# A fused attention and Fourier-filter kernel: the order of the prologue's last products, one eviction, the first queries and the first PV batch are rearranged

## The chip, the cores and the metric

The kernel runs on one core of one Trainium2 chip. The metric is the device time of one execution in microseconds. Lower is better. Three runs of the kernel before gave 673.25, 674.58 and 678.07 us, so the median is 674.58 us.

The engines of the core are named as the profile names them: PE is TensorE (matmuls; its weight loads are PEld), ACT is ScalarE, DVE is VectorE, POOL is GpSimd, SP is SyncE, which here issues most DMAs.

## The reference

Two results are computed from two inputs of 2048 rows by 448 columns and concatenated by columns.

```python
# A: attention, 16 query heads of width 28, one shared key and value head
q = (x @ wq).reshape(B, S, 16, 28).transpose(0, 2, 1, 3)
k, v = x @ wk, x @ wv
p = softmax(einsum("bhqd,bkd->bhqk", q, k) * 28 ** -0.5)
a = einsum("bhqk,bkd->bhqd", p, v) ... @ wo
# B: a spectral filter
y = irfft2(rfft2(x) * (w_r + 1j * w_i))
return concatenate([a, y], axis=-1)
```

## The kernel before, in words

The program has a prologue (about the first 71 us of the profiled execution), a branch, and a main loop of 256 steps.

**The prologue.** Queries, keys and values are projected in four column chunks of 512 (`proj`, L298; evicted by ACT into `qraw`, L302). Between the projections stand the first pieces of the Fourier transform: `fft1_fold` on DVE, `fft1_a(q)` (L120: 64 small products into two tiles `pa`, 32 for each `p`, each tile evicted by ACT into `a`, L123), and `fft1_b(q)`, which is `fft1_mm(q)` (L135: 16 products into `pbb` and `po`) followed by `fft1_out(q)` (eviction into `bs`, L143 on ACT or L147 on DVE for q = 7, then a store).

At the prologue's end PE has these left, in this order: `fft1_a(6)`, `fft1_b(5)`, `fft1_a(7)` whole, then small products: `shift(1, NC)` (L239, one product that sums the bounds `prod`), eight transposes of the values (`turn`, L401, into `pv`), four products of one row for the largest bound (L406, `pb3`), eight more transposes, and last `fft1_mm(6)`.

The chain that decides the branch runs over these engines: DVE computes `prod` (L235), PE does `shift`, DVE copies `cvec` (L240) and reduces it to `cmax` (L394), PE does the `pb3` products, DVE reduces them to `bits` (L407). Every engine loads `bits` into a register and branches on it (L412, L413). The branch holds a fallback for bounds over a limit. With this input it is not taken. On the path that is not taken, each of PE, ACT and DVE waits for its own earlier instructions to be done before it goes on.

**The first queries.** `build_q(0, 0, True)` scales the first query tile (`qt`, L185), rounds it (`qh`, L186) and takes the remainder (`ql`, L187), all on DVE. `copy_q` puts `qh` and `ql` into the tile `qa`: four copies of 32 partitions on DVE (L172) and four on ACT (L175). `twice(q, u)` (L165, DVE) then copies 64 partitions of one half u of `qa` to the other 64.

**After the branch.** ACT evicts the values from `pv` to `vs` (L444) and the two tiles of `fft1_mm(6)`. DVE makes the second half of the keys (`keys(1, ...)`, L228 and L229), then parts of the next query tile, and evicts `fft1_mm(7)` (L147).

**The main loop.** Each step makes two score tiles `s` (L694, two products each, three buffers of two PSUM banks), ACT exponentiates each into `p` (L697), and `flush` issues the products of `p` with the values (PV, L676, four for a step). `LAG = 1`: at each odd step `flush(1)` issues all waiting steps but one. So the first PV batch comes at step 3 and holds the steps 0 and 1; every later batch holds two steps as well. Step 0 has `fft1_b(7)` between its scores and those of step 1. `fft1_mm(7)` and the PV tile take the same PSUM buffer (`ps_o`, one buffer).

**What sets the order.** PE's order is the program's order, written by hand (`manual_schedule`). On ACT, DVE, POOL and SP a planner orders the instructions by its own estimate of when each can start; on the chip each engine then runs its list strictly in that order. `behind(a, b)` only fixes that `a` is listed after `b`; it adds no wait. PSUM tiles of the prologue come from a pool of six banks that is closed at the branch, and the score tiles take the same banks.

Of the kernel before, what the change touches and what calls it, by code (L numbers as in the profile page):

```python
# [9 lines left out]
F32 = mybir.dt.float32  # L10
# [3 lines left out]
AF = mybir.ActivationFunctionType  # L14
ALU = mybir.AluOpType
# [8 lines left out]
NC = 4  # L24
# [8 lines left out]
LAG = 1  # L33
# [5 lines left out]
def kernel(ctx: ExitStack, tc: tile.TileContext, t: dict):  # L39
    nc = tc.nc  # L40
# [12 lines left out]
    qraw = cp.tile([128, NG, S], F32, name="qraw")  # L53
    ka = cp.tile([128, S], F32R, name="ka")
    vs = cp.tile([128, 16, 32], F32, name="vs")
    cvec = cp.tile([128, NG, NC], F32, name="cvec")
# [4 lines left out]
    def behind(ins, other):  # L61

        tc.add_manual_dep(ins.ins, other.ins.name,
                          mybir.DependencyInfo(mybir.DependencyClass.NoSync, mybir.DependencyReason.DATA),
                          reason="order of issue")
# [12 lines left out]
    fc, xb, ff = {}, {}, {}  # L78
# [29 lines left out]

    at1, stored = {}, []

    def fft1_a(q):
        f, cs1 = ff.pop(q), fc["cs1"][:113]
        for p in range(2):
            pa = ps1[0].tile([128, 2, DF], F32, name="pa", tag="p")
            for e in range(2):
                for k, (n, o0) in enumerate(((113, 0), (112, 113))):
                    for h in range(2):
                        for r in range(2):
                            r0 = 64 * h + 32 * r
                            mm(pa[r0:r0 + 32, e, o0:o0 + n], f[:, 2 * r + k, 2 * p + e, h], cs1[:, 2 * r + k, :n],  # L120
                               start=True, stop=True)
            a = at1[q, p] = fp.tile([128, 2, DF], F32, name="a", tag=("pwr", "pwi")[p])
            nc.scalar.activation(a, pa, AF.Copy)  # L123
# [37 lines left out]

    qa = {}

    def twice(q, u):
        return nc.vector.tensor_copy(q[64:128, 2 * u:2 * u + 2], q[0:64, 2 * u:2 * u + 2].bitcast(F32))  # L165

    def copy_q(q, qh, ql, after=None, whole=True):

        for u in range(2):
            for i in (2 * u, 2 * u + 1):  # L170
                r = slice(32 * i, 32 * i + 32)
                v = nc.vector.tensor_copy(q[0:32, i], qh[r].bitcast(F32))  # L172
                if after is not None:
                    behind(v, after)
                a = nc.scalar.activation(q[32:64, i], ql[r].bitcast(F32), AF.Copy)  # L175
            if u == 0 or whole:
                v = twice(q, u)
        return a, v

    def build_q(c, g, first=False):  # L180
        cs = slice(c * CW, (c + 1) * CW)
        qt = qp.tile([128, CW], F32, name="qt", bufs=1)
        qh = qp.tile([128, CW], F32R, name="qh", bufs=1)
        ql = qp.tile([128, CW], F32R, name="ql", bufs=1)
        nc.vector.tensor_scalar(qt, qraw[:, g, cs], mask, cvec[:, g, c:c + 1], op0=ALU.mult, op1=ALU.add)  # L185
        nc.vector.tensor_copy(qh, qt)  # L186
        nc.vector.tensor_tensor(ql, qt, qh.bitcast(F32), op=ALU.subtract)  # L187
        if (c, g) not in qa:
            qa[c, g] = qp.tile([128, 4, CW], F32R, name="qa")
        q = qa[c, g]  # L190
        if first:
            return q, qh, ql
        for i in range(4):
            for p, src in enumerate((qh, ql)):
                mv = nc.sync.dma_start(q[32 * p:32 * p + 32, i].bitcast(F32), src[32 * i:32 * i + 32].bitcast(F32))
                behind(mv, stored[-1])
        nc.sync.dma_start(q[64:128].bitcast(F32), q[0:64].bitcast(F32))
# [7 lines left out]
    with tc.tile_pool(name="w1", bufs=1) as w1, tc.tile_pool(name="p1", bufs=6, space=PSUM) as p1:  # L205
# [28 lines left out]
        def terms(c0, c1):  # L234
            return nc.vector.tensor_scalar(prod[:, :, c0:c1], qmx[:, :, c0:c1], kmb, None, op0=ALU.mult)  # L235
# [151 lines left out]
            fetch(range(12, 14), slice(1536, S), nc.gpsimd)  # L387

        fft1_a(6)
        copy_q(*parts, terms(1, NC), False)  # L390
        fft1_b(5)
        fft1_a(7)
        shift(1, NC)
        top = nc.vector.tensor_reduce(cmax, cvec, axis=AX.X, op=ALU.max)  # L394
        behind(twice(parts[0], 1), top)

        pv = p1.tile([128, 16, 32], F32, name="pv", tag="p")

        def turn(bs):
            for b in bs:  # L400
                nc.tensor.transpose(pv[:, b], kf[32:64, b * 128:(b + 1) * 128], ident[32:64, 32:64])  # L401

        turn(range(8))
        pb3 = p1.tile([128, 64], F32, name="pb3", tag="p")
        for g in range(NG):
            mm(pb3[0:1, 4 * g:4 * g + 4], cmax[:, g:g + 1], sel4, start=True, stop=True)  # L406
        nc.vector.tensor_reduce(bits, pb3[0:1, 0:16], axis=AX.X, op=ALU.max)  # L407
        turn(range(8, 16))
        pb6 = fft1_mm(6)


# [1 line left out]
        with tc.If(rv > int(np.float32(BOUND).view(np.int32))), tc.tile_pool(name="g1", bufs=1) as g1:  # L413
            k4 = g1.tile([128, S], F32, name="k4")
            nc.vector.memset(k4, 0.0)
            for i in range(4):
                nc.vector.tensor_copy(k4[32 * i:32 * i + DH], kf[0:DH])
            mz = g1.tile([128, 4, 32], F32, name="mz")
            nc.vector.memset(mz, 0.0)


            qv = qraw.rearrange("p g (b q) -> p (g b) q", q=128)
            banks = [p1.tile([128, 512], F32, name="ps", tag="p") for _ in range(2)]
            with tc.For_i(0, 64, 1) as n:
                qs = g1.tile([128, 128], F32, name="qs")
                nc.vector.tensor_copy(qs, qv[:, bass.ds(n, 1)][:, 0])
                mx = g1.tile([128, 4, 4], F32, name="mx")
                for i in range(4):
                    r = slice(32 * i, 32 * i + 32)
                    for h in range(4):  # L430
                        ps = banks[0]
                        mm(ps, qs[r], k4[r, h * 512:(h + 1) * 512], start=True, stop=True)
                        nc.vector.tensor_reduce(mx[:, i, h:h + 1], ps, axis=AX.X, op=ALU.max)
                nc.vector.tensor_reduce(mz[:, :, DH], mx, axis=AX.X, op=ALU.max)
                pt = banks[1][:, :128]
                mm(pt, mz.rearrange("p i d -> p (i d)"), ident, start=True, stop=True)
                nc.vector.scalar_tensor_tensor(qs, qs, mask, pt, op0=ALU.mult, op1=ALU.add)
                nc.vector.tensor_copy(qv[:, bass.ds(n, 1)][:, 0], qs)
            nc.vector.memset(cvec, 0.0)
            nc.vector.memset(mask, 1.0)  # L440
            on_act, on_dve = copy_q(*build_q(0, 0, True))


        behind(nc.scalar.activation(vs, pv, AF.Copy), on_act)  # L444
        fft1_out(6, pb6, on_act)
        behind(keys(1, nc.vector.tensor_copy), on_dve)

# [220 lines left out]
    step = 0  # L668

    def flush(n, last=False):  # L670
        while len(pend) > n:
            c, g, kc, ps = pend.pop(0)
            if kc == 0:
                po[c, g] = ps_o.tile([128, CW], F32, name="po")
            for i in range(4):
                mm(po[c, g][32 * i:32 * i + 32], vs[:, kc], ps[i // 2][:, i % 2], start=(kc == 0), stop=(kc == 15))  # L676
            if kc == 15:
                o = osb[c, g] = ap.tile([128, CW], F32, name="osb")
                if last:
                    for k in range(4):  # L680
                        s = slice(128 * k, 128 * k + 128)
                        nc.scalar.activation(o[:, s], po[c, g][:, s], AF.Copy)
                else:
                    nc.vector.tensor_copy(o, po[c, g])  # L684
                    for k in range(4):
                        at(max(step + 1, 64 * c + 43) + k, norm, c, g, k)

    for n, (c, g) in enumerate(order):
        for kc in range(16):
            ps = []  # L690
            for u in range(2):
                s = ps_s.tile([128, 2, CW], F32, name="s")
                for j in range(2):
                    last = mm(s[:, j], ka[:, kc * 128:(kc + 1) * 128], qa[c, g][:, 2 * u + j], start=True, stop=True)  # L694
                begun.append(last)
                p = pp.tile([128, 2, CW], F32, name="p")
                nc.scalar.activation(p, s, AF.Exp, scale=SCALE)  # L697
                ps.append(p)
            if kc % 2 == 0:
                for f, a in between.pop(step // 2, []):  # L700
                    f(*a)
            else:
                flush(LAG)
            pend.append((c, g, kc, ps))
            for f, a in later.pop(step, []):
                f(*a)
            if kc == 4 and n + 1 < len(order):
                build_q(*order[n + 1])
            step += 1
# [4 lines left out]
    c = NC - 1  # L714
# [137 lines left out]
```

## Time and profile before

| what | us |
|---|---|
| median of three runs | 674.58 |
| the three runs | 673.25, 674.58, 678.07 |
| the profiled execution, whole | 674.18 |
| its span, first to last instruction | 672.3 |
| from the prologue's last projection to the first score | 64.17 to 71.80 |
| PE busy | 664.3 |
| ACT busy | 529.2 |
| DVE busy | 318.1 |

The profiled execution lies 0.40 us under the median and 1.9 us over its own span. A row of a timeline reads: start in us from the span's start, duration, engine, line, operation, the tile written and the tiles read, how many instructions the row merges, and in brackets how long the engine was idle before it and whom it waited for. A row of a stage table reads: the stretch, its length, and busy time with number of instructions of PE, PEld, DVE, ACT and POOL, then the granted TensorE clock as a share of the full one, the mean busy share of the DMA engines and GB/s.

### The profile page before, as it was taken

Reading aid. Unit: us, or ns where it says so; the run is one execution under the profiler, and the core shown is the slowest. Engines: PE = TensorE matmul, PEld = TensorE weight load, DVE = VectorE, ACT = ScalarE, POOL = GpSimd, SP = SyncE. Lnnn points to the kernel's source line nnn. Section 1 sums busy time; section 2 is a strip of 40 time slices with the busy share of each in tenths; the row PEclk is TensorE's granted clock in tenths of the full one; section 3 lists DMA queues with packets and bytes.
Section 4 is the critical chain, followed back from the end, with each engine's and each line's share of the span. In section 5 each row is a group of like instructions: output and inputs, shape, how many; then the busy total and the mean of one; then the engine's idle time right before and its main releaser. Section 6 shows DMA issues by size and latency. Waiting matters only on the chain.

```text
span 672.3 us, 11826 instructions
## 1 busy us (share of the span) xinstructions
PE 664.3 (99%) x4480; PEld 370.6 (55%) x4480; DVE 318.1 (47%) x769; ACT 529.2 (79%) x607; POOL 62.6 (9%) x113
## 2 busy tenths in 40 slices
PE   9999999999999999999999999999999999999997
PEld 6877544555555555555555555555555555555555
DVE  6999438659895902055332502072614220171513
ACT  4555888888888888888888888888888888888881
POOL 3022261111110000000011100000100100000110
PEclk9999899999999999999999999999999999999999
DMA  8755785555551323030322311020424130120001
GB/s 275 248 169 166 205 208 144 135 142 141 139 145 41 78 82 78 15 77 15 105 72 62 88 49 43 25 65 17 132 58 100 50 76 15 46 59 1 28 29 56
DMA packets 34251, 61.87 MB, mean 92 GB/s; under 512 B 6529, under 2 KB 22802, under 8 KB 33228
## 3 DMA queue, kind: packets, MB, share of 16 engines
q1 hardware_dynamic: 30544, 49.18, 26.4%
q0 software_dynamic: 3072, 11.00, 6.5%
q8 instruction: 36, 0.59, 0.4%
q10 hardware_dynamic: 576, 0.92, 0.4%
q14 instruction: 23, 0.19, 0.1%
HBM read 29.35 MB, written 14.75 MB: 66 GB/s over the span
## 4 chain that ended last, share of the span: by engine, by line
PE 87%; ACT 1%; issue 0%; ACTq 0%
PE s L694 39%; PE po L676 35%; PE pw L596 5%; PE py L558 2%; PE pz L544 2%; ACT p L697 1%; PE s L596 1%; PE pc L463 1%; PE pu L465 0%; PE pc L464 0%; PE pc L465 0%; PE pu L463 0%; PE pu L464 0%; ACT yb L601 0%; PE pbb L135 0%
## 5 line engine op out<-in xcount | busy, mean ns | idle before, releaser
L697 ACT ACTIVATE p<-s 128x1024 f32<-128x1024 f32 x512 | 484.9, 1031 | 96.5 <-PE s L694 96.5
L694 PE MATMUL s<-qa,ka 128*128 128x512 f32 x1024 | 300.4, 415 | 2.1 <-ACT p L697 1.5
L694 PEld LDWEIGHTS s<-qa,ka 128*128 128x128 f32 x1024 | 177.9, 189 | 140.2 <-ACT p L697 114.9
L676 PE MATMUL po<-p,vs 128*32 128x512 f32 x2048 | 246.0, 598 | 0.0
L676 PEld LDWEIGHTS po<-p,vs 128*32 128x32 f32 x2048 | 53.6, 109 | 123.6 <-issue 118.2
L603 DVE COPY ya<-pw 128x448 f32<-128x448 f32 x12 | 7.5, 625 | 145.2 <-PE pw L596 127.7
L584 DVE RECIPROCAL r<-r 128x128 f32<-128x128 f32 x64 | 60.8, 950 | 1.2
L564 DVE TENSOR_TENSOR y<-py,m 128x226 f32<-128x226 f32 x16 | 6.3, 394 | 64.0 <-ACT m L562 64.0
L547 DVE COPY z<-pz 113x512 f32<-113x512 f32 (+1 forms) x16 | 11.1, 692 | 48.6 <-PE pz L544 48.6
L536 POOL DMA_DIRECT2D fi<-fi x8 | 4.4, 551 | 246.2 <-PE pz L544 239.6
L567 POOL TENSOR_TENSOR yo<-y 128x226 f32<-128x226 f32 x16 | 9.3, 583 | 188.4 <-issue 174.6
L298 PE MATMUL pq<-xh,wqh 128*128 128x512 f32 x64 | 26.2, 409 | 0.5 <-ACT wqh L280 0.5
L298 PE MATMUL pq<-xh,wql 128*128 128x512 f32 x64 | 25.3, 396 | 0.1
L491 DVE CAST bh<-b 128x450 fp32r<-128x450 f32 x16 | 6.4, 397 | 38.7 <-PE pu L464 21.1
L302 ACT ACTIVATE qraw<-pq 128x512 f32<-128x512 f32 x16 | 9.2, 600 | 18.0 <-PE pq L298 18.0
L684 DVE COPY osb<-po 128x512 f32<-128x512 f32 x15 | 10.4, 690 | 20.9 <-PE po L676 20.9
L298 PE MATMUL pq<-xl,wqh 128*128 128x512 f32 x48 | 19.1, 397 | 0.0
L583 DVE STREAM_SHUFFLE r<-osb 128x128 f32<-128x128 f32 x64 | 19.0, 297 | 0.1
L585 DVE TENSOR_TENSOR osb<-osb,r 128x128 f32<-128x128 f32 x64 | 18.4, 288 | 1.2
L596 PE MATMUL pw<-woh,ol 128*128 128x448 f32 x51 | 18.8, 368 | 0.0
L596 PE MATMUL pw<-wol,oh 128*128 128x448 f32 x51 | 18.6, 365 | 0.0
L596 PE MATMUL pw<-woh,oh 128*128 128x448 f32 x51 | 18.5, 362 | 0.0
(124 smaller groups left out, 568.3 us busy)
## 6 DMA issues: line engine op xcount, KB each, us to landing
qa<-qa SPq DMA_DIRECT2D x15, 512.0 KB, 4.2
raw<-xa SPq DMA_DIRECT2D x16, 256.0 KB, 5.2
xb<-xb SPq DMA_DIRECT2D x8, 512.0 KB, 3.6
qa<-qh SPq DMA_DIRECT2D x60, 64.0 KB, 2.0
qa<-ql SPq DMA_DIRECT2D x60, 64.0 KB, 2.0
ob<-yo SPq DMA_DIRECT2D x16, 226.0 KB, 2.2
t<-bs SPq DMA_DIRECT2D x16, 225.0 KB, 4.6
wr<-wr POOLq DMA_DIRECT2D x16, 225.0 KB, 4.8
```

Source lines behind the costliest of these rows:

```text
L298: mm(pq, w[:, j, gs], x[:, j], start=(j == 0 and n == 0), stop=(j == 3 and n == 1))
L544: mm(pz[:w, j], c2["c", q][:, j, o0:o0 + w], c2["F", q][:, j], start=True, stop=True)
L547: nc.vector.tensor_copy(z[:w], pz[:w].rearrange("p j (r n) -> p r j n", r=2))
L558: mm(py[:, k], z[:w, r, js], cs3[:w, k], start=True, stop=True)
L583: nc.vector.stream_shuffle(r, o, [DH] * 32)
L584: nc.vector.reciprocal(r, r)
L585: nc.vector.tensor_tensor(o, o, r, op=ALU.mult)
L596: mm(p, x[c][:, g, s], w[:, g], start=(g == 0 and n == 0), stop=(g == NG - 1 and n == 2))
L676: mm(po[c, g][32 * i:32 * i + 32], vs[:, kc], ps[i // 2][:, i % 2], start=(kc == 0), stop=(kc == 15))
L684: nc.vector.tensor_copy(o, po[c, g])
L694: last = mm(s[:, j], ka[:, kc * 128:(kc + 1) * 128], qa[c, g][:, 2 * u + j], start=True, stop=True)
L697: nc.scalar.activation(p, s, AF.Exp, scale=SCALE)
```

## The change

Four edits, in the order of the diff:

- `fft1_a` takes a list of halves, so that the halves p = 0 and p = 1 of `fft1_a(7)` can be issued apart.
- `copy_q` handles one half u at a time; `twice` is called apart from it. `build_q(..., first=True)` makes `qt` and `qh` on ACT; `ql` stays on DVE.
- The prologue's end is reordered. PE's new order: `fft1_b(5)`, `shift(1, NC)`, `fft1_a(7)` half 0, the `pb3` products, all sixteen transposes, `fft1_a(7)` half 1, `fft1_mm(6)`. ACT evicts `vs` before the branch, between the evictions of the two halves of `fft1_a(7)`. `twice(0)` is listed behind `cmax`; `copy_q(1)` and `twice(1)` follow in the program without such a rule.
- `flush(LAG if step > 1 else 0)`: at step 1 the PV products of step 0 are issued. The batch at step 3 then holds step 1 alone. From step 5 on the batches are as before.

```diff
-    def fft1_a(q):
-        f, cs1 = ff.pop(q), fc["cs1"][:113]
-        for p in range(2):
+    def fft1_a(q, ps=range(2)):
+        f, cs1 = ff[q], fc["cs1"][:113]
+        for p in ps:
...
+    def copy_q(u, q, qh, ql):
+        for i in (2 * u, 2 * u + 1):
+            r = slice(32 * i, 32 * i + 32)
+            v = nc.vector.tensor_copy(q[0:32, i], qh[r].bitcast(F32))
+            a = nc.scalar.activation(q[32:64, i], ql[r].bitcast(F32), AF.Copy)
+        return a, v
...
-        nc.vector.tensor_scalar(qt, qraw[:, g, cs], mask, cvec[:, g, c:c + 1], op0=ALU.mult, op1=ALU.add)
-        nc.vector.tensor_copy(qh, qt)
+        if first:
+            nc.scalar.activation(qt, qraw[:, g, cs], AF.Identity, bias=cvec[:, g, c:c + 1], scale=mask)
+            nc.scalar.activation(qh, qt, AF.Copy)
+        else:
+            nc.vector.tensor_scalar(qt, qraw[:, g, cs], mask, cvec[:, g, c:c + 1], op0=ALU.mult, op1=ALU.add)
+            nc.vector.tensor_copy(qh, qt)
...
         fft1_a(6)
-        copy_q(*parts, terms(1, NC), False)
+        ts = terms(1, NC)
+        behind(copy_q(0, *parts)[1], ts)
         fft1_b(5)
-        fft1_a(7)
         shift(1, NC)
         top = nc.vector.tensor_reduce(cmax, cvec, axis=AX.X, op=ALU.max)
-        behind(twice(parts[0], 1), top)
-        pv = p1.tile([128, 16, 32], F32, name="pv", tag="p")
-        def turn(bs):
-            for b in bs:
-                nc.tensor.transpose(pv[:, b], kf[32:64, b * 128:(b + 1) * 128], ident[32:64, 32:64])
-        turn(range(8))
+        behind(twice(0, *parts), top)
+        copy_q(1, *parts)
+        twice(1, *parts)
+        fft1_a(7, (0,))
         pb3 = p1.tile([128, 64], F32, name="pb3", tag="p")
         for g in range(NG):
             mm(pb3[0:1, 4 * g:4 * g + 4], cmax[:, g:g + 1], sel4, start=True, stop=True)
         nc.vector.tensor_reduce(bits, pb3[0:1, 0:16], axis=AX.X, op=ALU.max)
-        turn(range(8, 16))
+        pv = p1.tile([128, 16, 32], F32, name="pv", tag="p")
+        for b in range(16):
+            nc.tensor.transpose(pv[:, b], kf[32:64, b * 128:(b + 1) * 128], ident[32:64, 32:64])
+        nc.scalar.activation(vs, pv, AF.Copy)
+        fft1_a(7, (1,))
         pb6 = fft1_mm(6)
...
-        behind(nc.scalar.activation(vs, pv, AF.Copy), on_act)
...
-                flush(LAG)
+                flush(LAG if step > 1 else 0)
```

In the changed program as it is built, the lists of the engines differ from those before in these places alone. On DVE the part in question reads: `ql`, a copy of `qh`, the reduction of the last `qraw`, a copy of `qh`, `prod`, two copies of `qh`, `twice(1)`, `cvec`, `cmax`, `twice(0)`, `bits`. Its `twice(1)` waits for the last of ACT's four copies of `ql`. On ACT the part reads: the last `qraw`, two copies of `ql`, a tile of `fft1_a(6)`, a copy of `ql`, the other tile of `fft1_a(6)`, a copy of `ql`, two tiles of `fft1_mm(5)`, half 0 of `fft1_a(7)`, `vs`, half 1 of `fft1_a(7)`, the branch. Before, DVE's list read: `prod`, three copies of `qh`, `twice(0)`, a copy of `qh`, `cvec`, `cmax`, `twice(1)`, `bits`.

More of the change, by code (lines that the diff above doesn't have):

```diff
@@ L162, with twice @@
     qa = {}
[L164 to L178, printed above, removed]
+    def copy_q(u, q, qh, ql):
[4 more added lines that the diff above has]
+        return a, v
+    def twice(u, q, *_):
+        return nc.vector.tensor_copy(q[64:128, 2 * u:2 * u + 2], q[0:64, 2 * u:2 * u + 2].bitcast(F32))
     def build_q(c, g, first=False):
@@ L440 @@
             nc.vector.memset(mask, 1.0)
-            on_act, on_dve = copy_q(*build_q(0, 0, True))
-        behind(nc.scalar.activation(vs, pv, AF.Copy), on_act)
+            parts = build_q(0, 0, True)
+            for u in range(2):
+                on_act, _ = copy_q(u, *parts)
+                on_dve = twice(u, *parts)
         fft1_out(6, pb6, on_act)
```

## The prediction

> **What bounds the kernel now.** I read the page first, then the busy time by stage around the branch, then the timelines of PE, ACT and DVE there.
>
> ```profile
> span 672.3 us, 11826 instructions
> ...
> PE 87%; ACT 1%; issue 0%; ACTq 0%
> ```
>
> The chain that ended last is PE's for 87% of the span. The changed lines all run before step 6 of the main loop, that is before about 88 us, and from step 5 on the loop is the same. So the change is worth what it adds or takes on PE's path between the last projection and the first regular PV batch.
>
> ```profile
> 64.78:68.19 3.41, 3.41 (x124) 2.83 (x116) 3.28 (x8) 2.94 (x6) 1.00 (x2) 1.00 0.59 192
> 68.19:71.60 3.41, 3.05 (x54) 2.25 (x45) 1.80 (x6) 3.22 (x8) 0.00 (x0) 1.00 0.13 29
> 71.60:75.02 3.42, 3.22 (x20) 1.95 (x20) 3.15 (x5) 2.66 (x4) 2.74 (x5) 0.50 0.94 222
> 75.02:78.43 3.41, 3.04 (x18) 1.65 (x10) 1.76 (x4) 2.47 (x4) 2.06 (x4) 1.00 1.00 247
> ...
> 75.28:81.47 6.19, 5.64 (x32) 2.36 (x28) 1.54 (x3) 5.42 (x6) 2.06 (x4) 1.00 1.03 293
> ```
>
> The column after the five engines is the granted clock. From 71.60 to 75.02 it is half. The stretch before it, as long, held mostly small products; the one before that held only Fourier products and was followed by the full clock. In the last row PE waits 6.19 - 5.64 = 0.55 us.
>
> ```profile
> 66.70 1.75 PE L120 MATMUL pa<-cs,f 113*32 113x113 f32 x64
> ...
> 68.38 0.39 PE L239 MATMUL pb<-prod,blk 128*128 128x12 f32 x2
> 68.70 0.68 PE L401 MATMUL pv<-ident,kf 32*128 32x32 f32 x8
> 69.33 0.34 PE L406 MATMUL pb<-sel,cmax 128*1 128x4 f32 x8
> 69.61 0.71 PE L401 MATMUL pv<-ident,kf 32*128 32x32 f32 x8
> 70.25 0.41 PE L135 MATMUL pbb<-a,fw 64*64 64x225 f32 x2
> ...
> 70.88 0.36 PE L135 MATMUL po<-a,fw 64*64 64x225 f32 x2
> 71.80 2.04 PE L694 MATMUL s<-qa,ka 128*128 128x512 f32 x4 [0.56 <-ACT vs L444]
> 73.78 0.64 PE L135 MATMUL pbb<-a,fw 64*64 64x225 f32 x2
> ...
> 75.28 1.66 PE L694 MATMUL s<-qa,ka 128*128 128x512 f32 x6
> ...
> 79.62 1.92 PE L676 MATMUL po<-p,vs 128*32 128x512 f32 x16
> ```
>
> From 66.70 to 70.88 + 0.36 = 71.24 PE runs without a gap: 4.54 us. Then 0.56 us pass before the first scores.
>
> **Part by part. First the new wait on PE.** These are ACT's and DVE's rows.
>
> ```profile
> 64.20 0.60 ACT L302 ACTIVATE qraw<-pq 128x512 f32<-128x512 f32 x1 [1.79 <-PE pq L298]
> ...
> 65.77 1.27 ACT L175 ACTIVATE qa<-ql 32x512 fp32r<-32x512 f32 x2
> 67.07 0.55 ACT L123 ACTIVATE a<-pa 128x450 f32<-128x450 f32 x1
> 67.63 1.27 ACT L175 ACTIVATE qa<-ql 32x512 fp32r<-32x512 f32 x2
> ...
> 70.94 0.60 ACT L444 ACTIVATE vs<-pv 128x512 f32<-128x512 f32 x1 [0.16 <-ACTq L413]
> ```
>
> ```profile
> 61.44 0.16 DVE L240 COPY cvec<-pb 128x4 f32<-128x4 f32 x1
> ...
> 62.17 0.69 DVE L103 TENSOR_TENSOR xb<-f 113x512 f32<-113x512 f32 x1
> 62.77 0.54 DVE L185 TENSOR_SCALAR qt<-qraw,mask,cvec 128x512 f32<-128x512 f32 x1
> 63.23 0.42 DVE L104 TENSOR_TENSOR f<-xb 113x256 f32<-113x256 f32 x1
> ...
> 64.57 0.42 DVE L186 CAST qh<-qt 128x512 fp32r<-128x512 f32 x1
> 65.03 0.69 DVE L187 TENSOR_TENSOR ql<-qt,qh 128x512 fp32r<-128x512 f32 x1
> 65.64 0.68 DVE L303 TENSOR_REDUCE qmx<-qraw 128x1 f32<-128x512 f32 x1
> 66.35 0.23 DVE L235 TENSOR_SCALAR prod<-qmx,kmb 128x12 f32<-128x12 f32 x1
> 66.49 1.28 DVE L172 CAST qa<-qh 32x512 fp32r<-32x512 f32 x3
> ...
> 68.83 0.15 DVE L240 COPY cvec<-pb 128x12 f32<-128x12 f32 x1
> 69.02 0.17 DVE L394 TENSOR_REDUCE cmax<-cvec 128x4 f32<-128x16 f32 x1
> 69.22 0.69 DVE L165 CAST qa<-qa 64x1024 fp32r<-64x1024 f32 x1
> 69.94 0.16 DVE L407 TENSOR_REDUCE bits<-pb 1x1 f32<-1x16 f32 x1
> 71.77 0.68 DVE L228 CAST ka<-kf 32x1024 fp32r<-32x1024 f32 x1 [1.67 <-DVEq L413]
> ...
> 76.20 0.62 DVE L147 COPY bs<-po 128x450 f32<-128x450 f32 x1
> ```
>
> The nearest row for `qt` and `qh` on ACT is a copy of the same shape, from the groups by line and form:
>
> ```profile
> L288 ACT ACTIVATE xh<-raw 128x512 fp32r<-128x512 f32 x12 | 7.1, 626 | 0.2
> ```
>
> Without L185 and L186, DVE takes the four folds (64.57 - 63.23 = 1.34 us) right after L103 ends at 62.86, so about 62.92 to 64.26, and `ql` runs 64.26 to 64.95. ACT makes `qt` and `qh` between its evictions before that. `qt` needs the first columns of `cvec`, which are there at 61.60. Two instructions of 0.626 us are 1.25 us, and ACT is idle for 1.79 us ahead of the `qraw` eviction at 64.20. So I take them as hidden, with `qh` done by about 63.7. A scale and a bias read per partition are not in that copy; at 0.9 us each (the two would just fill 1.79) they would still end before `ql` can start. If ACT had not this idle time, their 1.25 us would stand ahead of everything below. DVE then has two copies of `qh` (1.28/3 = 0.43 each) and the reduction (0.68) ahead of `prod`: 64.87 + 0.43 + 0.68 + 0.43 = 66.4, where it is now (66.35). Nothing is gained there.
>
> ACT starts its copies of `ql` at 65.0 and works through four of them and two tiles of `fft1_a(6)`: 4 x 0.635 + 2 x 0.55 = 3.64, so the last ends at about 68.7. DVE's `twice(1)` is listed ahead of `cvec` and waits for that last copy. All of DVE's bound chain is queued behind it. So `twice(1)` runs 68.75 to 69.44, `cvec` starts at 69.4, `cmax` 0.19 later, and it is done at about 69.75, not 69.19. Now `cvec` at 68.83 needs only PE's shift.
>
> PE meanwhile does `shift` when `prod` is done (66.75, 0.32 to the next product by 68.38 and 68.70) and half of `fft1_a(7)` (1.75/2 = 0.88), so it stands at 67.95 before the `pb3` products, which need `cmax`. They start at 69.85: 1.9 us of idle PE that does not exist now. The products left are the same ones as now, so the prologue ends at 71.24 + 1.9 to 1.95, about 73.2, and the first scores come at about 73.75. Bounds: `pb3` follows ACT's last copy by 1.15 us (68.7 to 69.85), and DVE's own copies end at 67.35 (66.49 + 2 x 0.43), so 0.5 us of wait is left even if ACT is no limit; 2.3 if `qt` and `qh` push `ql` by 0.4. I take 1.95, from the rows as they stand.
>
> **`vs` ahead of the branch.** The gap of 0.56 is put down to `vs`, which ends at 70.94 + 0.60 = 71.54; the rest is issue. PE also has its own branch in that gap. In the built program the first scores wait for ACT's path through the branch, which now lies behind the eviction of half 1. ACT passed the branch in 0.16 (its row), DVE in 1.67. I expect at most 0.3 (71.24 to 71.54), at least 0; I take 0, because PE's branch fills it.
>
> **The clock.** Four scores and `fft1_mm(7)` take 75.28 - 71.80 = 3.48 us now. At full clock `fft1_mm` takes 71.24 - 70.25 = 0.99, and four scores about 0.95 (six issue within 1.66, which includes the last one's end). So the half clock costs 3.48 - 1.94 = 1.53. With the change the stretch from 68.19 to 71.60 holds 1.65 us of idle, then `pb3` and sixteen transposes (0.3 + 1.3), and next to nothing dense, less than the stretch that led to half clock now. So I expect half clock from 71.60 again. It then covers half 1 of `fft1_a(7)`, `fft1_mm(6)` (75.28 - 73.78 = 1.50 at half clock against 0.99: 0.5 lost) and the first scores up to 75.02 (0.3 lost): 0.8 plus some for half 1, together 0.95.
> [...]
>
> So step 1's scores start at 75.28 + 1.95 - 1.53 + 0.95 = 76.65, 1.4 later than now.
>
> **The first PV batch.** Four of the eight products of the 1.92 us row move ahead of step 2's scores, while ACT catches up. The 0.55 us of waits can go. Against that, the first PV now comes before DVE has emptied the bank that `fft1_mm(7)` used: 76.82 by the last DVE row, and `bits` is 0.5 later in the change (`twice(0)` 69.75 to 70.44, then `bits`), so about 77.5. Step 1's scores end at 76.65 + 0.95 = 77.6, so this wait is hidden in the forecast; if the clock stays full, the scores end near 76.7 and PE waits 0.8. Bounds -0.55 and +0.3 net; I take -0.5, since the wait is covered.
>
> **Sum.** 1.95 - 1.53 + 0.95 - 0.5 = 0.9 us. On the profiled execution's own 674.18 (672.3 of span and 1.9 around it): **675.1 us**. The median of the runs is 0.40 above that execution, so against 674.58 this is half a microsecond, a change of 0.1%. About 1%, 6.7 us, is what a measurement can tell from no change.
>
> **Rivals.** *ACT's copies are no limit, and the clock stays full* (faster). The wait is 0.5, PE has dense work on both sides of the small products, and 1.53 is gained. `pb3` stands at 68.45, 0.9 before its present 69.33, so `bits` and DVE's work after the branch are 0.9 earlier and L147 ends at 75.9. Step 1's scores start at 75.28 + 0.5 - 1.53 = 74.25 and end at 75.2, so the first PV waits 0.7 for L147 against the 0.55 that goes. Sum: 0.5 - 1.53 + 0.15 = -0.9, 673.3 us; without any wait of PV 672.6. For it: the shorter light part. Against it: 3.64 us of ACT rows. Chance 0.14.
>
> *The wait is there, but no half clock follows.* This rests on the phase of the 3.41 us stretches against the program: if a border falls at 69.7, each side holds about half of the 3.5 us (1.9 + 0.3 + 1.3) light part. Then step 1's scores start at 75.28 + 1.95 - 1.53 = 75.7, the first PV waits 0.8 for DVE against 0.55 of waits that go, and the sum is 0.42 + 0.25 = +0.7: 674.9 us. [...] Chance 0.2.
>
> *A second stretch at half clock* (slower). If the stretch 71.60 to 75.02, with 0.5 us of branch and 64-row products at half speed, also counts as light, half clock lasts to 78.43. It decides where PE's dense share is under what 71.60 to 75.02 has now (3.22 busy). Another 3.41/2 = 1.7 is lost: +2.6, 676.8 us. Chance 0.12.
>
> *The change does nothing measurable*, all gains and losses covered: 674.2. Chance 0.04.
>
> **Numbers.** The forecast has 0.5. All five cases lie between 672.6 and 676.8, and the runs before spread from 1.3 under to 3.5 over their median. The range is 673.0 to 677.6. None of the cases reaches 1%, so "within 1%" gets 0.96; slower 0.025, for several light stretches in a row; faster 0.015.
>
> **What would show it.** In the changed profile: PE idle of about 1.9 us before the `pb3` products, put down to `cmax`; `twice(1)` starting about when ACT's fourth copy ends, near 68.7; the first scores near 73.8 to 74.5; a stage of 3.4 us at clock 0.50; the first PV of four products ahead of step 2, with or without a wait for L147; the regular batches from step 5 about 0.9 us later than now. It is wrong if `cvec` starts before 68.5, or if the PE gap before `pb3` is under 1 us.

## The result, and the profile after

| | before | changed |
|---|---|---|
| median of 16 runs each | 673.59 | 676.87 |
| lowest and highest | 672.28, 678.07 | 674.56, 679.2 |
| the profiled execution | 674.18 | 676.22 |
| its span | 672.3 | 674.4 |

The ratio is 1.0045 (95%: 1.0029 to 1.006): the changed kernel is slower by about 3.3 us, half a percent. First the stage table of the changed kernel, in the stretches of 3.41 us in which the granted clock changes (columns as before: stretch, length, PE, PEld, DVE, ACT, POOL, clock, DMA share, GB/s):

```profile
64.87:68.29 3.42, 2.81 (x78) 1.96 (x70) 2.16 (x6) 3.34 (x6) 0.90 (x2) 1.00 0.49 154
68.29:71.70 3.41, 2.09 (x52) 1.97 (x56) 1.88 (x5) 2.02 (x5) 0.00 (x0) 1.00 0.32 63
71.70:75.11 3.41, 2.84 (x33) 1.47 (x23) 2.39 (x4) 1.56 (x4) 2.23 (x4) 0.50 0.47 122
75.11:78.53 3.42, 3.42 (x21) 1.76 (x20) 1.85 (x4) 1.94 (x2) 2.85 (x6) 0.50 1.01 247
```

Two stretches are at half clock, where the profile of the kernel before had one. Over the sixteen runs of the changed kernel the time goes with the mean clock: 674.56 us at 0.996, 677.15 to 679.2 at 0.991, with one exception (678.17 at 0.995). The timeline of PE in the same profile:

```profile
66.70 0.98 PE L120 MATMUL pa<-cs,f 113*32 113x113 f32 x32
69.50 0.34 PE L401 MATMUL pb<-sel,cmax 128*1 128x4 f32 x8 [1.82 <-DVE cmax L393]
69.95 1.15 PE L406 MATMUL pv<-ident,kf 32*128 32x32 f32 x16
71.03 1.16 PE L120 MATMUL pa<-cs,f 113*32 113x113 f32 x32
72.12 0.64 PE L135 MATMUL pbb<-a,fw 64*64 64x225 f32 x2
...
73.31 0.58 PE L135 MATMUL po<-a,fw 64*64 64x225 f32 x2
74.46 2.04 PE L696 MATMUL s<-qa,ka 128*128 128x512 f32 x4 [0.57 <-PEq L413]
...
78.15 1.35 PE L696 MATMUL s<-qa,ka 128*128 128x512 f32 x4
79.47 1.07 PE L678 MATMUL po<-p,vs 128*32 128x512 f32 x8
...
86.63 1.93 PE L678 MATMUL po<-p,vs 128*32 128x512 f32 x16
```

PE stands for 1.82 us before the one-row products, for `cmax`. `fft1_mm(6)` then takes 73.89 - 72.12 = 1.77 us (0.99 before), the four scores of step 0 take 2.04. Who holds `cmax` is in the timeline of DVE:

```profile
66.29 0.85 DVE L168 CAST qa<-qh 32x512 fp32r<-32x512 f32 x2
68.36 0.69 DVE L173 CAST qa<-qa 64x1024 fp32r<-64x1024 f32 x1 [1.22 <-ACT qa L169]
69.08 0.17 DVE L239 COPY cvec<-pb 128x12 f32<-128x12 f32 x1
69.28 0.17 DVE L393 TENSOR_REDUCE cmax<-cvec 128x4 f32<-128x16 f32 x1
```

and in that of ACT:

```profile
62.69 0.63 ACT L182 ACTIVATE qh<-qt 128x512 fp32r<-128x512 f32 x1
63.88 0.60 ACT L301 ACTIVATE qraw<-pq 128x512 f32<-128x512 f32 x1 [0.56 <-PE pq L297]
...
67.70 0.63 ACT L169 ACTIVATE qa<-ql 32x512 fp32r<-32x512 f32 x1
```

DVE is idle for 1.22 us because `twice(1)` (L173) waits for ACT's last copy, which ends at 68.33, and the bound (`cvec`, `cmax`) is queued behind it. `qt` and `qh` on ACT are hidden: 0.56 us of idle time is left before the next eviction.

When the last projection ends differs between profiles (62.7 to 65.7 us in the fourteen of this case, already so at the second chunk), so profiles are compared from there. To the first regular PV batch (84.04 before, 86.63 after) it is 19.88 us before and 22.79 after: +2.91. Of these +2.98 arise up to the first scores, +0.21 between the scores of steps 0 and 1, and -0.28 from there to that batch. From that batch to the end of the span the changed kernel takes 0.5 less (587.75 against 588.23), so the spans lie 2.1 apart.

### The profile page after: what moved, and what is told of

It is laid out like the page before. It is cut to its first block, busy times and chain, and to the rows that moved or that the text cites. A ratio compares the mean times of both kernels' runs of the same rounds, so it can differ in the third digit from the quotient of the medians.

```text
span 674.4 us, 11823 instructions
## 1 busy us (share of the span) xinstructions
PE 665.2 (99%) x4480; PEld 370.4 (55%) x4480; DVE 317.5 (47%) x767; ACT 530.5 (79%) x609; POOL 63.2 (9%) x113
## 4 chain that ended last, share of the span: by engine, by line
PE 87%; ACT 1%; issue 0%; ACTq 0%
PE s L696 39%; PE po L678 35%; PE pw L598 5%; PE py L560 2%; PE pz L546 2%; ACT p L699 1%; PE s L598 1%; PE pc L465 0%; PE pu L467 0%; PE pc L466 0%; PE pc L467 0%; PE pu L466 0%; PE pu L465 0%; ACT yb L603 0%; PE pbb L135 0%
```

## The experiments

All were timed in five rounds, in three sessions of four kernels, each session on one chip with the kernel before beside them (its medians: 673.19 for e1 to e4, 673.07 for e5 to e8, 673.04 for e9 to e12). Each kernel has 12 runs, e2 and e3 have 6. The table puts them side by side. A and B are the delays of steps 6 and 16 of the main loop in the profiled execution, counted from the end of the last projection and against the second profile of the kernel before (e9); "half" is the number of stretches at half clock before 105 us.

| kernel | ratio to before (95%) | A | B | half |
|---|---|---|---|---|
| before, first profile | | 1.49 | 1.55 | 1 |
| e9, before again | 0.9997 (0.9977 to 1.0018) | 0 | 0 | 0 |
| changed | 1.0045 (1.0029 to 1.006) | 4.40 | 4.34 | 2 |
| e1, `twice(1)` behind `cmax` | 1.0021 (1.0009 to 1.0033) | 3.24 | 3.34 | 2 |
| e2, late PV | 1.0074 (1.005 to 1.0098) | 3.45 | 4.19 | 1 |
| e3, gap filled | 1.0049 (1.0033 to 1.0066) | 2.88 | 2.91 | 0 |
| e4, e1 and late PV | 1.0016 (0.9998 to 1.0034) | 3.31 | 3.20 | 2 |
| e5, e1 and transposes split | 1.0011 (0.9993 to 1.0029) | 0.94 | 2.61 | 0 |
| e6, e5 and late PV | 1.0023 (0.9999 to 1.0046) | 0.14 | 3.82 | 1 |
| e7, before with early PV | 1.0009 (0.9987 to 1.0032) | 2.67 | 2.56 | 1 |
| e8, before with queries on ACT | 1.0033 (1.0015 to 1.0051) | 0 | 5.17 | 1 |
| e10, e5 with transfers held | 0.9998 (0.9982 to 1.0014) | 1.00 | 0.89 | 0 |
| e11, e8 with transfers held | 1.0004 (0.9985 to 1.0023) | 0 | -0.07 | 0 |
| e12, changed with queries on DVE | 1.0017 (0.9999 to 1.0036) | 3.27 | 3.16 | 2 |

**e1: the wait for `cmax` taken away.**

```diff
-        twice(1, *parts)
+        behind(twice(1, *parts), top)
```

> The changed kernel with one rule more: DVE's twice(1) is listed behind cmax too, so cvec and cmax no longer wait for ACT's last copy of ql. My theory (the 1.82 us PE gap before the pb3 products comes from that order, and it is what feeds the half clock): the gap falls under 0.3 us, bits come about 1 us earlier, at most one half-clock stretch of 3.4 us is left before 80 us, and the time falls by 1.5 to 3.3 us against the changed kernel, to the level of the kernel before or below it. Rival (the transposes in one row are what lowers the clock, with or without a gap): the gap goes but two half-clock stretches stay, and the time falls by no more than 1.6 us.

674.53 us, ratio 1.0021: about half of the loss goes with the wait, 2.3 us, as the theory had it. PE's timeline in e1:

```profile
68.08 0.98 PE L120 MATMUL pa<-cs,f 113*32 113x113 f32 x32
68.88 0.35 PE L401 MATMUL pb<-sel,cmax 128*1 128x4 f32 x8
69.30 0.90 PE L406 MATMUL pv<-ident,kf 32*128 32x32 f32 x12
70.80 0.40 PE L406 MATMUL pv<-ident,kf 32*128 32x32 f32 x4 [0.60 <-DMA kf<-qraw]
```

The gap before the one-row products is gone. A wait that the gap had covered comes out: the last four transposes need the last columns of `kf`, which a transfer brings. Two stretches at half clock stayed in this profile, as the rival had it, though nine of the twelve runs had a mean clock of 0.999 or 1.0. Those nine have a median of 674.18, still 1.0 above the runs of the kernel before at 0.998 or more in that session (673.16). So what e1 keeps of the loss is not the half clock alone.

**e2 and e4: the first PV batch put back**, in the changed kernel and in e1.

```diff
-                flush(LAG if step > 1 else 0)
+                flush(LAG)
```

> The changed kernel with the first PV batch as before (steps 0 and 1 together at step 3). My theory (the early PV of step 0 fills time in which PE would wait for ACT): 0.3 to 0.5 us slower than the changed kernel. Rival (the early PV has to wait for DVE's eviction of the last Fourier product and costs time): 0.3 to 0.8 us faster.

> The changed kernel with twice(1) behind cmax and the first PV batch as before. My theory: with the gap gone and the clock fuller, step 1's scores end before DVE has emptied the bank for PV, so here the late PV is no worse than the early one: the same as the run with twice(1) behind cmax alone within 0.4 us, or faster by as much. Rival (the early PV always fills ACT's lag): 0.3 to 0.5 us slower than that run.

e2 gave 678.01, e4 674.75. In the changed kernel the late batch is slower (1.0074 against 1.0045, the intervals overlap a little), in e1 it makes no difference (1.0016 against 1.0021). So the early batch does not cause the loss. That it saves something while PE is at half clock is likely but not shown: e2 has six runs, and its profiled execution, 674.88, is the lowest of them, so its A and B in the table do not stand for its median.

**e3: the gap filled.** Fourteen products that nothing reads stand ahead of `pb3`.

```diff
+        nothing = p1.tile([128, 512], F32, name="nothing", tag="p")
+        dense = ident.bitcast(BF16)
+        for _ in range(14):
+            mm(nothing[:, :256], dense[:, :128], dense, start=True, stop=True)
```

> The changed kernel with 14 idle products (128x128 by 256, bf16, result unused) in PE's gap before the pb3 products; the order on DVE and ACT and so the wait stays. My theory (the gap lets the clock go to half and that costs more than the gap itself): the clock stays full or has at most one half-clock stretch, and the time falls by 1 to 2 us although cmax comes no earlier. Rival (the wait is all that costs): no change beyond 0.3 us.

The timeline of PE in e3:

```profile
68.91 1.70 PE L402 MATMUL nothing<-ident 128*128 128x256 bf16 x14
70.92 0.34 PE L405 MATMUL pb<-sel,cmax 128*1 128x4 f32 x8 [0.31 <-DVE cmax L393]
...
74.94 1.17 PE L700 MATMUL s<-qa,ka 128*128 128x512 f32 x4 [0.57 <-DVE ka L227]
...
79.23 1.07 PE L682 MATMUL po<-p,vs 128*32 128x512 f32 x8 [1.07 <-DVE bs L147]
```

With the gap filled by work of no use no stretch of this profile is at half clock, and four scores take 1.17 us in place of 2.04. So the idle time had a part in the half clock, as far as one profile shows it: three of the six runs, at 0.996 or 0.997, still had some. Of the gain, 1.07 us go to a new wait: the first PV batch comes before DVE has emptied the bank of `fft1_mm(7)`. The profile is 1.5 us better (A 2.88 against 4.40), the median only 0.4 (676.45) where 1 to 2 was expected. So a gain from filling the gap is not shown.

**e5 and e6: the light run (one-row products and transposes) cut in two**, on e1; e6 has the late PV batch as well.

```diff
         for b in range(16):
+            if b == 8:
+                fft1_a(7, (1,))
             nc.tensor.transpose(pv[:, b], kf[32:64, b * 128:(b + 1) * 128], ident[32:64, 32:64])
         nc.scalar.activation(vs, pv, AF.Copy)
-        fft1_a(7, (1,))
```

> The changed kernel with two edits: the second doubling (L173) stands behind the maximum cmax on DVE, and the 16 transposes stand in two groups of 8 around the last half of fft1_a(7), with the four one-row products pb3 still ahead of them. Theory (the loss is the 1.82 us for which PE waited for cmax, and the light run of pb3 and 16 transposes, 1.5 us in one piece, that kept PE at half clock for a second stretch of 3.41 us): with no wait and the light run cut into pieces of 1.0 and 0.6 us, and with the last four transposes 1.2 us later, so that the 0.60 us wait for the transfer of kf that the run e1 showed is gone, the profile shows at most one half-clock stretch and the time from the last projection to the first regular PV batch falls from 21.6 us (e1) to 20.0 to 20.6; ratio to the kernel before 0.999 to 1.0012. Rival (what e1 kept of the loss lies in the order of the three blocks itself, or in the early PV batch, not in the light run): ratio as in e1, 1.002, and that stretch of time 21.3 us or more.

> As e5_split, with the first PV batch of step 1 put back to its old place (LAG at every step). Theory: at full clock the early PV batch waits for the rest of the keys' copies on DVE (1.07 us in the run e3) and is worth nothing or costs up to 0.5 us, at half clock it saves 0.3 to 0.5 us. If the split gives the full clock, this kernel is 0 to 0.5 us below e5_split, ratio to the kernel before 0.998 to 1.001. Rival (an early PV batch always saves): 0.3 to 0.5 us above e5_split.

e5: 673.81, ratio 1.0011, no half clock in the profile, a mean clock of 0.999 or 1.0 in all 12 runs, and no wait for `kf`. From the last projection to the first regular PV batch it takes 19.33 us, less than the 20.0 to 20.6 expected. The stage table of e5 and, below it, PE's timeline:

```profile
72.77:76.18 3.41, 2.20 (x24) 1.10 (x20) 2.86 (x6) 3.29 (x4) 2.72 (x6) 1.00 0.88 232
76.18:79.59 3.41, 3.22 (x20) 1.50 (x16) 0.00 (x0) 2.00 (x3) 0.17 (x1) 1.00 1.04 336
```

```profile
75.82 1.06 PE L679 MATMUL po<-p,vs 128*32 128x512 f32 x8 [1.21 <-DVE bs L147]
...
95.86 0.44 PE L466 MATMUL pu<-bh,g1h 128*128 128x450 f32 x1 [0.97 <-DVE bh L494]
```

e6: 675.06, where 0 to 0.5 under e5 was expected; a miss. At step 6 both stand as expected (A 0.94 and 0.14: with the late batch there is no wait for L147). Then, at the first product of the second transform stage, both meet a wait for `bh` (0.97 us in e5, 1.71 in e6), and in e6's profile half clock follows it. B, 2.61 and 3.82, shows it.

**e7: the early PV batch alone, in the kernel before.**

```diff
-                flush(LAG)
+                flush(LAG if step > 1 else 0)
```

> The kernel before with the early PV batch of step 1 alone. Theory: the kernel before runs this place at full clock in most runs, so the PV batch meets a wait for DVE in place of work: ratio 1.000 to 1.0015. Rival (early PV saves whatever the clock): 0.9993 or below, 0.5 us less than before.

673.94, 1.0009: as expected, though the interval holds both cases. The timeline of PE in its profile shows the wait:

```profile
75.33 1.20 PE L694 MATMUL s<-qa,ka 128*128 128x512 f32 x4
78.41 1.76 PE L676 MATMUL po<-p,vs 128*32 128x512 f32 x8 [1.88 <-DVE bs L147]
```

In this profile, at a clock of 1.00 up to 78.65, the early batch buys PE 1.88 us of idle time, and a stretch at 0.50 (78.65 to 82.06) comes after it.

**e8: the queries on ACT alone, in the kernel before.** The edit is that of `build_q` in the change.

> The kernel before with the first queries' scaling and rounding (qt, qh) on ScalarE alone. Theory: both lie beside the prologue's projections with slack on each side, so the ratio is 0.9993 to 1.0007. Rival (the two copies on ScalarE hold up the evictions of the projections that are queued behind them, by their 1.44 us): ratio 1.001 to 1.002, and PE waiting for ScalarE in the last projections.

675.74, 1.0033: neither of the two, though near the second in size. Nothing is lost from the last projection to step 6 (A is 0), and that projection ends at 62.67, earlier than in the other thirteen profiles, so the copies hold up no projection. The loss is later. PE's timeline in e8:

```profile
91.76 1.20 PE L698 MATMUL s<-qa,ka 128*128 128x512 f32 x4
96.20 0.44 PE L467 MATMUL pu<-bh,g1h 128*128 128x450 f32 x1 [3.25 <-DVE bh L495]
```

and its stage table:

```profile
93.52:96.94 3.42, 0.73 (x3) 0.41 (x4) 1.08 (x3) 1.01 (x2) 0.00 (x0) 1.00 1.05 185
96.94:100.35 3.41, 3.41 (x13) 1.70 (x17) 3.06 (x5) 1.90 (x2) 2.04 (x3) 0.50 0.68 151
```

PE waits 3.25 us for DVE's `bh`, DVE for the load of `b`, and half clock follows. In that stretch the DMA engines are fully busy (share 1.05).

**e9: the kernel before, unchanged.**

> The kernel before, unchanged, for a second profile of it and as a measure of what its runs scatter. Theory (the profile of the kernel before on which the prediction rests had a half-clock stretch that most of its timed runs, at a mean clock of 0.999 to 1.0, do not have; without it PE arrives some 1.4 us earlier at the first product of the second transform stage, L463, and meets there a wait for the loads of b, which land 22 to 25 us after the branch whatever PE does): ratio 0.9985 to 1.0015, clock 0.999 or 1.0, 19.88 us from the last projection to the first regular PV batch become 18.4 to 18.6, and PE waits 0.5 to 3 us at L463. Rival (the half-clock stretch is in its usual run too): 19.9 us, and no wait at L463.

672.86, 0.9997. The stage table and, below it, PE's timeline of this second profile:

```profile
66.51:69.92 3.41, 3.41 (x94) 2.89 (x87) 3.27 (x9) 3.34 (x7) 0.00 (x0) 1.00 0.14 41
69.92:73.33 3.41, 2.84 (x35) 1.86 (x38) 1.73 (x5) 3.01 (x7) 1.38 (x3) 1.00 0.59 145
```

```profile
66.76 1.75 PE L120 MATMUL pa<-cs,f 113*32 113x113 f32 x64
...
70.28 0.41 PE L135 MATMUL pbb<-a,fw 64*64 64x225 f32 x2
...
71.83 1.17 PE L694 MATMUL s<-qa,ka 128*128 128x512 f32 x4 [0.57 <-ACT vs L444]
...
94.36 0.36 PE L463 MATMUL pu<-bh,g1h 128*128 128x450 f32 x1
```

The same program, instruction for instruction, without half clock. Its stretches of 3.41 us lie 1.7 us earlier against the program than in the first profile, so that the light run is shared between two of them. From the last projection to the first regular PV batch it takes 1.49 us less. The wait at L463 that I expected is not there: DVE made `bh` at 93.58, 0.8 us ahead of PE. That half of the expectation failed.

**e10 and e11: transfers held back**, on e5 and e8. GpSimd reads one element of `bh` once it is there, and its transfers that nothing needs yet are listed behind that. The constants of the third transform stage (`cs3`) are issued at step 14 in place of step 1.

```diff
+        if u == 0:
+            one = fp.tile([1, 1], F32, name="one", bufs=1)
+            landed.append(nc.gpsimd.tensor_copy(one, bh[0:1, 0, 0:1].bitcast(F32)))
...
-                behind(ld, begun[0])
+                behind(ld, landed[0] if q else begun[0])
...
-        nc.gpsimd.dma_start(w, t["wo"][:, g])
+        behind(nc.gpsimd.dma_start(w, t["wo"][:, g]), landed[0])
```

> The kernel e5_split, with GpSimd's transfers that nothing needs yet (wr and wi of the later quarters, cs3, wo, fi) held back behind the first load of b: GpSimd first reads one element of bh. Theory (the wait of 0.97 to 3.25 us for bh in e5, e6 and e8 is that load, which shares the DMA engines, busy all through that stretch, with these transfers): b<-t takes 3 to 6 us from issue to bh in place of 9.5, the wait at L466 is gone, and the 0.55 us that e5 had gained on the kernel before by then, and lost there, stay: ratio 0.9970 to 0.9995. Rival (the load takes its 9 us by itself): the wait stays within 0.5 us, ratio as in e5, 1.001.

> The kernel e8_before_q_on_act with the same transfers held back. Theory (the 2.2 us that e8 lost are the 3.25 us for which PE waited for bh and the half-clock stretch that followed that idle time, not the queries' copies): with the wait gone, ratio 0.9965 to 0.9995, 2.5 us or more below e8. Rival (the copies on ScalarE cost by themselves): ratio as in e8, 1.0025 to 1.004.

e10: 673.04, 0.9998. e11: 673.48, 1.0004. The wait for `bh` is gone in both. The load's issue on SP's queue in e8,

```profile
85.41 1.78 SPq L480 DMA_DIRECT2D b<-t  x4
```

comes 10.25 us before DVE starts on it:

```profile
95.66 0.40 DVE L495 CAST bh<-b 128x450 fp32r<-128x450 f32 x1 [20.34 <-DMA b<-t]
```

In e11 the load is issued at 82.73, since the store that it waits for lands sooner too, and DVE starts on it at 87.51, 4.78 us later:

```profile
82.73 2.65 SPq L480 DMA_DIRECT2D b<-t  x4
```

```profile
87.51 0.40 DVE L495 CAST bh<-b 128x450 fp32r<-128x450 f32 x1 [10.68 <-DMA b<-t]
...
103.97 2.96 DVE L513 CAST ph<-pwr 128x450 fp32r<-128x450 f32 x1 [0.72 <-PE pc L468]
```

So the load had been slow because of the transfers that now start behind it. The medians fell by 2.3 us from e8 to e11 (the intervals still overlap) and by 0.8 from e5 to e10, less than expected. In both profiles about 1 us is given back between 106 and 126 us: DVE's copy to `ph` takes 2.96 us in e11 (0.40 in e9), while GpSimd splits `wo` (L462 and L463, 103.38 to 106.67), which it now does later, and PE then waits 0.3 us for `bh`. But both profiles have won that back by the end of the span (against e9, e10 is 0.89 late at step 16, 2.0 at step 20 and 0.85 at the end, e11 -0.07, 0.75 and -0.30), so it does not explain why the medians fell by less, and this stays open. Neither kernel is faster than the one before; e10 is its equal.

**e12: the changed kernel with the queries back on DVE.**

```diff
-        if first:
-            nc.scalar.activation(qt, qraw[:, g, cs], AF.Identity, bias=cvec[:, g, c:c + 1], scale=mask)
-            nc.scalar.activation(qh, qt, AF.Copy)
-        else:
-            nc.vector.tensor_scalar(qt, qraw[:, g, cs], mask, cvec[:, g, c:c + 1], op0=ALU.mult, op1=ALU.add)
-            nc.vector.tensor_copy(qh, qt)
+        nc.vector.tensor_scalar(qt, qraw[:, g, cs], mask, cvec[:, g, c:c + 1], op0=ALU.mult, op1=ALU.add)
+        nc.vector.tensor_copy(qh, qt)
```

> The changed kernel with the first queries' scaling and rounding back on VectorE, all else as changed. Theory (on ScalarE they lie in idle time; what e8 lost by them was the wait for bh that an earlier PE met, and the changed kernel is too late to meet it): as the changed kernel, ratio to the kernel before 1.0035 to 1.0055. Rival (the copies on ScalarE cost 2.2 us by themselves, in the changed kernel too): ratio 1.0005 to 1.002.

674.92, 1.0017: the rival's number, for another reason. DVE's timeline in e12:

```profile
67.82 0.15 DVE L235 COPY cvec<-pb 128x12 f32<-128x12 f32 x1
68.01 0.17 DVE L389 TENSOR_REDUCE cmax<-cvec 128x4 f32<-128x16 f32 x1
68.20 0.69 DVE L173 CAST qa<-qa 64x1024 fp32r<-64x1024 f32 x1
68.92 0.16 DVE L398 TENSOR_REDUCE bits<-pb 1x1 f32<-1x16 f32 x1
69.76 0.69 DVE L173 CAST qa<-qa 64x1024 fp32r<-64x1024 f32 x1 [0.67 <-ACT qa L169]
```

`twice(1)` now stands last. No rule of `behind` puts it there; the planner does, which lists DVE's work otherwise once DVE has `qt` and `qh` to make. PE's wait for `cmax` shrinks to 0.28 us, and e12 behaves as e1, in time and in its two half-clock stretches.

## Why the prediction was partly right

**The wait for `cmax`: right.** 1.95 was forecast and 1.82 came, by the steps that were given: ACT's copies to 68.33 (68.7), `twice(1)` from 68.36 (68.75), `cmax` from 69.28 (69.6), in a profile whose last projection ends 0.32 earlier. e1 and e12 remove most of it in two ways, and each takes about half of the loss. What the prediction did not see is which edit it hangs on: it held the queries on ACT to cost nothing, and as work they do, but with them, and without a rule for `twice(1)`, the planner lists it ahead of the bound on DVE.

**`vs` ahead of the branch: right.** The gap before the first scores is 0.57 us in place of 0.56, now put down to PE's own branch.

**The clock: the step that failed.** "So the half clock costs 3.48 - 1.94 = 1.53" is confirmed: e9 without it is 1.49 shorter. "So I expect half clock from 71.60 again" came, from 71.70. But the sum then let it end at 75.02, "together 0.95", net -0.58. It lasted to 78.53. In the profile the half clock's terms are +0.21 for half 1 of `fft1_a(7)` (1.09 against 0.88 to the next product), +0.78 for `fft1_mm(6)` and +0.21 from step 0's scores to step 1's, where a gain of 1.53 had been booked: +1.2 in place of -0.58. With 1.82, 0.17 that is left over in the light products around them and -0.28 at the end, that is the +2.91. The case was among the rivals, "A second stretch at half clock (slower)", at 676.8 us and chance 0.12, with the rule that it decides where the stretch has less than 3.22 us of busy PE. It had 2.84. (That border is too high: in e2 a half-clock stretch with 2.97 returned to full.) Measured: 676.22 in the profiled execution, 676.87 in the median. That the median is so near to 676.8 is luck, since the rival was added up on a profiled execution of 674.18 and the median of the kernel before came out at 673.59. That it lies in the range is owed to the rivals that made the range wide: the forecast itself was +0.9, and +3.3 came.

**The early PV batch: right in sign in the profile, too large.** -0.5 was taken, -0.28 came, with the wait for L147 just covered: L147 ends at 79.42 and the batch starts at 79.47. That it would wait at full clock was said (0.8 us); e3, e5 and e7 show 1.07, 1.21 and 1.88.

**The base.** The forecast was made against a profiled execution that had the half clock, 674.18. (Its 675.1 was then set beside the median 674.58, which is 0.40 higher than that execution; the change that it forecast was 0.9 us and not the half microsecond that it names.) One stretch of 3.41 us at half clock takes 0.0025 from the mean clock over the span (3.41/2/672); the first profiled execution of the kernel before, with one up to 105 us, has 0.997, the second, with none, 1.0. Of the 93 runs of the kernel before in the three sessions 55 have a mean clock of 0.998 or more, so more than half have no such stretch, and neither has the second profile (672.56). In each session the median of these lies 1.2 to 1.9 us under that of the others. The changed kernel had 0.991 to 0.996 in all of its 16 runs. So the gain of 1.53 that the prediction booked could not be had in most runs, and the medians lie 3.3 us apart where the two profiles lie 2.0.

Left open: what e1 and e12 keep of the loss in the runs at full clock (in the profile of e5, at full clock, PE's waits for L147 and `bh` are left); why the copies on ACT made the load of `b` late in e8 (in e8 the transfers of `wo` and `fi` start 0.7 us ahead of it, in e9 2.1, and this is as far as the traces go); and whether the kernel before gains by the held transfers, which was not tried.

## What to carry to other kernels

Where a short light stage stands between dense ones, ask what the clock will do behind it and how long it lasts, and take a second profile of the kernel before: the kernel before ran this place at a clock of 0.50 in its first profile and at 1.00 in e9, and a gain booked against the rarer case is not there. With the light run cut into pieces between dense work (e5) the mean clock was 0.999 or 1.0 in all twelve runs. In one piece it was so in nine of twelve without the wait for `cmax` (e1) and in none of sixteen with it (the change, 0.991 to 0.996). When one operation goes to another engine, look at how the list of the engine that it left is put together, and at the next transfer that an earlier PE will meet: there e6 and e8 lost 3.7 and 5.2 us in their profiles (B less A).

## What the runs showed of the hardware

**Where the clock went to half.** In these profiles the half clock begins and ends at borders 3.41 us apart (71.60 and 75.02 in the first profile of the kernel before, 71.70 and 78.53, two stretches later, in that of the changed one), so cut the span there (in profiles without one before 105 us, count back from the half clock that follows the span's end; in the first profile of the kernel before that one begins at 672.35, 175 stretches after 75.02). In each stretch count the time in which PE has projection, Fourier, score or PV products (in e3 the products of no use too), and leave out the transposes, the shift's narrow products and the one-row ones. By the rows shown, the stretch before the half clock has 0.67 us of it in the changed kernel (71.03 to 71.70), and 1.25 in the first profile of the kernel before (66.70 + 1.75 - 68.19 = 0.26, and 70.25 to 71.24), though PE was busy there for 3.05. In e9 the two stretches have 2.00 (to 68.51) and 2.49 (70.28 to 71.27, 71.83 to 73.33), and the clock stayed at 1.00. Counted so over the fourteen profiles up to 100 us, the eight stretches of 1.59 us or less were all followed by half clock; four from 1.65 to 1.70 went three times to full and once to half (1.70 in e6); all from 1.90 (e3) up went to full. So in these fourteen profiles the two kinds meet between 1.59 and 1.90 us. At half clock, four with PE busy for 2.80 to 2.84 us stayed at half (changed, e1, e4 and e12), and nine with 2.97 or more returned to full. PE's whole busy and idle time does not tell the stretches apart: in e5 1.21 us idle and 2.20 busy, all with dense work, were followed by full clock, in the first profile of the kernel before 0.36 idle and 3.05 busy by half.

**Where the stretches lie differed between two executions of the same program**: the one that holds the last transposes of the kernel before starts at 68.19 in its first profile and at 69.92 in e9, with the last projection ending at the same time (64.16 and 64.22).

**In e5 the full clock helped as far as the next transfer**: PE was 0.94 us late at step 6, waited 0.97 for `bh` and was 2.61 late at step 16. The load of `b` takes 6.6 us to `bh` in e9 and 10.25 in e8, with the same order of transfers on SP's and GpSimd's queues and a DMA share of 0.89 to 1.05 in the stretches of 3.41 us between. With the other transfers held back it takes 4.78 in e11, at a share of 0.59.
